# The prologue of a fused attention and MLP kernel: K and V from one combined weight, key norms from ScalarE, LayerNorm statistics and normalisations shared out anew over the engines

## The chip, the cores and the metric

The kernel runs on 1 core of one Trainium2 chip. The metric is the time of one execution in device microseconds (us), as the median of several executions. The profiler's own span of an execution is about 2 us shorter than the time measured for it, so spans are compared with spans and times with times.

Engine names: PE is TensorE (PEld its weight loads), ACT is ScalarE, DVE is VectorE, POOL is GpSimd, SP is SyncE.

## The reference

One LayerNorm feeds two branches, multi-query attention (32 query heads of width 16, one K and V head) and an MLP with GELU. Both are added to the input.

```python
S, D, H, Dh, F = 2048, 512, 32, 16, 1792           # bfloat16 inputs
def reference(A_x, A_wq, A_wk, A_wv, A_wo, B_x, B_w1, B_b1, B_w2, B_b2):
    def _A_ref(x, wq, wk, wv, wo):
        q = (x @ wq).reshape(B, S, H, Dh).transpose(0, 2, 1, 3)
        k = x @ wk
        v = x @ wv
        scores = einsum("bhqd,bkd->bhqk", q, k) * (Dh ** -0.5)
        p = softmax(scores, axis=-1)
        o = einsum("bhqk,bkd->bhqd", p, v)
        return o.transpose(0, 2, 1, 3).reshape(B, S, H * Dh) @ wo
    def _B_ref(x, w1, b1, w2, b2):
        return gelu(x @ w1 + b1) @ w2 + b2
    x = A_x
    xn = layernorm(x, eps=1e-5)                    # no scale, no shift
    return x + _A_ref(xn, ...) + _B_ref(xn, ...)
```

## The kernel before

The program is a list of operations with due dates. A scheduler, run when the kernel is built, fixes the order of the operations of each engine; semaphores come from the dependencies. So each engine has one fixed order. An operation that is ready still waits if the one ahead of it on its engine is not.

An eviction, below, is an operation that copies a result of TensorE from `pAll` (PSUM, the memory that its matmuls write to) to a tile such as `xnT` or `KT`. A filler is a matmul on zeros that only keeps TensorE busy. `bn_stats` are the statistics of a tile of rows, `ve_b` its variances (plus 1e-5), `rstd` their inverse square roots, `nmr` is -mean * rstd.

The work falls into a prologue and a stream. The prologue loads x, normalises it, transposes it into `xnT`, projects K and V for all 16 tiles of 128 rows and Q for the first group of heads. The stream then computes scores, exponentials and the products with V, block by block, with the other projections and the MLP in the gaps of TensorE. It starts with the first exponential (`exp`).

Softmax needs a number to subtract from the scores. The kernel uses a bound on |q|·|k|: the largest squared norm of a key (`R2`) times the squared norm of each query. The square root of the product is taken by halving the bits of the float, in the operation that writes `QT`. So no exp can start before all 16 tiles are normalised, transposed and projected to K.

The parts that the change touches (cuts marked):

```python
Q_DUE = 20.0
XN_ENG = "dddddddpdpdpdpdd"        # who normalises each tile: d VectorE, p GpSimd
LN_B = ((0,2),(2,3,1),(3,6),(6,7,1),(7,10),(10,11,1),(11,14),(14,16))  # ",1": statistics on ScalarE
# ... TR_B, K_B: batches of the transposes and of the K projections
dma("act", wk_s[:], ...); dma("act", wv_s[:], ...); dma("act", wq_s, ...)
# ...
def ln_batch(ts, on_act):
    # ... on_act: two passes of ScalarE over the tile (Identity and Square with accumulation)
    for ti in () if on_act else ts:
        dve(lambda e, ti=ti: e.bn_stats(stats[:, ti, :], x_sb[:, ti, :]), ...)
    for ti in () if on_act else ts:
        dve(lambda e, ti=ti: e.bn_aggr(mv[:, ti, :], stats[:, ti, :]), ...)
    if not on_act:
        dve(lambda e: e.tensor_scalar(ve_b[:, sl], mv[:, sl, 1], 1e-5, None, ALU.add), ...)
    act(lambda e: e.activation(std_b[:, sl], ve_b[:, sl], ACT.Sqrt), ...)
    dve(lambda e: e.reciprocal(rstd[:, sl], std_b[:, sl]), ...)
    for ti in ts:
        # VectorE if XN_ENG[ti] == "d", else GpSimd:
        # tensor_scalar(xn[:, ti % 8, :], x_sb[:, ti, :], mean, rstd, subtract, mult)

def x_T(ts, bk, eng):   # 4 transposes a tile on TensorE, then one copy of 128x1024 to xnT
    # ... ScalarE if eng == "a", else VectorE

def k_proj(ts, bk):     # wkp: wk, four times side by side
    for d in range(DT):
        mm(bank(bk)[:, 0:n], wkp[:, d, :, :].rearrange(...), xnT[:, d, c], d == 0, d == DT - 1, ...)
    act(lambda e: e.activation(KT[:, c], bank(bk)[:, 0:n], ACT.Identity, bias=krow[:, 0:1], scale=GAM), ...)

def k_max(ts, bk):      # squared key norms: square, matmul with ones, maximum
    dve(lambda e: e.tensor_tensor(sqk[:, i % 2, 0:n], KT[0:Dh, c], KT[0:Dh, c], ALU.mult), ...)
    mm(bank(bk)[:, 0:n], ones[0:Dh, :], sqk[:, i % 2, 0:n], True, True, ...)
    dve(lambda e: e.tensor_reduce(kmax[:, i:i + 1], bank(bk)[:, 0:n], AX.X, ALU.max), ...)

def wq_first():         # the weights of the first group of heads, an eighth of wq
    setup(lambda e: e.tensor_copy(wqp[:, :, 0:4, 0:Dh], wq_s[:, :, 0:64].rearrange(...)), due=9.0)  # GpSimd
# ... v_tiles: V of each tile from wv_s into pO (16 columns a tile)

# the tail: the bound, then the first QT
dve(lambda e: e.tensor_reduce(R2[:], kmax[:, 0:nkm[0]], AX.X, ALU.max), ...)
dve(lambda e: e.tensor_scalar(selrR[:], selr[:], R2[:, 0:1], 1.03, ALU.mult, ALU.mult), ...)
mm(bank(7), selrR[...], sqq[...], False, True, ...)                     # adds |q|^2 R2 to row 16
dve(lambda e: e.tensor_scalar(QT[:, hq, :].bitcast(i16), bank(7).bitcast(i32), isc[:, 0:1], ibi[:, 0:1],
                              ALU.mult, ALU.add), ...)                  # halves the bits: square root
# then V1, Vf (VectorE), the scaled copies of V and the rest of wqp (GpSimd), and the stream
```

Of the kernel before, what the change touches and what calls it, by code (L numbers as in the profile page):

```python
# [10 lines left out]
P = 128  # L11
# [31 lines left out]
LP = 154  # L43
# [7 lines left out]
KM_DUE = 5.0  # L51
Q_DUE = 20.0
XN_ENG = "dddddddpdpdpdpdd"
LN_B = ((0,2),(2,3,1),(3,6),(6,7,1),(7,10),(10,11,1),(11,14),(14,16))
TR_B = (((0,2),0,"a"),((2,4),1,"a"),((4,6),2,"a"),((6,8),3,"a"),((8,10),0,"a"),((10,12),1,"a"),((12,14),2,"a"),((14,16),3,"a"))
K_B = (((0, 4), 4, 5), ((4, 8), 4, 5), ((8, 12), 4, 5), ((12, 14), 4, 5), ((14, 16), 0, 1))
# [356 lines left out]
def bass_parallel_sum__grouped_kv_mqa__dense_activation_gelu__prompt_kernel(  # L413
# [34 lines left out]
    with ExitStack() as es:  # L448
# [8 lines left out]
        wk_s = sb([P, DT, Dh], bf, "wk_s")  # L457
        wv_s = sb([P, DT, Dh], bf, "wv_s")
# [23 lines left out]
        selrR = sb([P, 4, 32], bf, "selrR")  # L482
# [3 lines left out]
        nm = sb([P, NT], f32, "nm")  # L486
        scr = sb([P, D], bf, "scr")
# [4 lines left out]
        sqk = sb([Dh, 2, TBW], bf, "sqk")  # L492
        kmax = sb([P, 8], f32, "kmax")
# [63 lines left out]
        dma("act", wk_s[:], A_wk.rearrange("(k p) n -> p k n", p=P), "d_wk", w=["wk_s"], due=0.0)  # L557
        dma("act", wv_s[:], A_wv.rearrange("(k p) n -> p k n", p=P), "d_wv", w=["wv_s"], due=0.0)
# [6 lines left out]
        def setup(fn, r=(), w=(), occ=0.25, due=0.0, **kw):  # L565
# [17 lines left out]
        setup(lambda e: e.tensor_copy(wkp[:, :, :, 0:Dh], wk_s[:].unsqueeze(2).to_broadcast([P, DT, 4, Dh])),  # L583
              r=["wk_s", "wkp"], w=["wkp"], occ=0.45, due=2.0)

        sel_diag = bass.AP(sel8[:].tensor, sel8[:].offset, [list(sel8[:].ap[0]), [33, 8], [8, 4]])
# [4 lines left out]
        setup(lambda e: e.tensor_scalar(ibi[:], mrow[:], float(0x1fc00000) / 65536.0, None, ALU.mult),  # L591
              r=["mrow"], w=["ibi"], due=10.0)
# [6 lines left out]

        def land(ti):  # L600
            return 3.0 + 1.2 * (ti // 2) + 0.3 * (ti % 2)

        def ln_batch(ts, on_act):
            sl, b = slice(ts[0], ts[-1] + 1), ts[0]
            d = land(ts[-1])
            for ti in ts if on_act else ():
                act(lambda e, ti=ti: e.activation(scr[:], x_sb[:, ti, :], ACT.Identity, accum_out=sm[:, ti:ti + 1]),
                    r=[("x", ti)], w=["scr", ("sm", ti)], n=TBW + 200, due=land(ti))
            if on_act:
                setup(lambda e: e.tensor_scalar(mv[:, sl, 0], sm[:, sl], 1.0 / D, None, ALU.mult),  # L610
                      r=[("sm", ti) for ti in ts], w=[("mv", b, ti) for ti in ts])
                setup(lambda e: e.tensor_scalar(nm[:, sl], sm[:, sl], -1.0 / D, None, ALU.mult),
                      r=[("sm", ti) for ti in ts], w=[("nm", ti) for ti in ts])
            for ti in ts if on_act else ():
                act(lambda e, ti=ti: e.activation(scr[:], x_sb[:, ti, :], ACT.Square, bias=nm[:, ti:ti + 1],
                                                  accum_out=sm[:, ti:ti + 1]),
                    r=[("x", ti), ("nm", ti)], w=["scr", ("sm", ti)], n=TBW + 200, due=land(ti))
            if on_act:
                setup(lambda e: e.tensor_scalar(ve_b[:, sl], sm[:, sl], 1.0 / D, 1e-5, ALU.mult, ALU.add),
                      r=[("sm", ti) for ti in ts], w=[("ve", b)])  # L620
            for ti in () if on_act else ts:
                dve(lambda e, ti=ti: e.bn_stats(stats[:, ti, :], x_sb[:, ti, :]), r=[("x", ti)], w=[("st", ti)],  # L622
                    due=land(ti) + 1.0)
            for ti in () if on_act else ts:
                dve(lambda e, ti=ti: e.bn_aggr(mv[:, ti, :], stats[:, ti, :]), r=[("st", ti)], w=[("mv", b, ti)], n=130,
                    due=d + 1.0)
            if not on_act:
                dve(lambda e: e.tensor_scalar(ve_b[:, sl], mv[:, sl, 1], 1e-5, None, ALU.add),
                    r=[("mv", b, ti) for ti in ts], w=[("ve", b)], n=30, due=d + 1.1)
            act(lambda e: e.activation(std_b[:, sl], ve_b[:, sl], ACT.Sqrt), r=[("ve", b)], w=[("std", b)], n=70, due=0.0)  # L630
            dve(lambda e: e.reciprocal(rstd[:, sl], std_b[:, sl]), r=[("std", b)], w=[("rstd", b)], n=30, due=d + 1.2)
            for ti in ts:
                eng = XN_ENG[ti]
                if eng == "d":
                    dve(lambda e, ti=ti: e.tensor_scalar(xn[:, ti % 8, :], x_sb[:, ti, :], mv[:, ti, 0:1],
                                                         rstd[:, ti:ti + 1], ALU.subtract, ALU.mult),
                        r=[("x", ti), ("rstd", b), ("mv", b, ti)], w=[("u", ti % 8)], mode=4, due=land(ti) + 2.0)
                else:
                    add("pool", lambda e, ti=ti: e.tensor_scalar(xn[:, ti % 8, :], x_sb[:, ti, :], mv[:, ti, 0:1],  # L639
                                                                 rstd[:, ti:ti + 1], ALU.subtract, ALU.mult),  # L640
                        [("x", ti), ("rstd", b), ("mv", b, ti)], [("u", ti % 8)], occ=0.76, lat=0.15, due=land(ti) + 2.0)

        def x_T(ts, bk, eng):
            n = len(ts)
            pT = bank(bk)[:, 0:n * 256].bitcast(bf)
# [26 lines left out]
        nkm = [0]  # L672

        def k_max(ts, bk):
            c = slice(ts[0] * P, (ts[-1] + 1) * P)
            n = len(ts) * P
            u = land(ts[-1]) + KM_DUE
            i = nkm[0]
            nkm[0] += 1
            dve(lambda e: e.tensor_tensor(sqk[:, i % 2, 0:n], KT[0:Dh, c], KT[0:Dh, c], ALU.mult),  # L680
                r=[("KT", ti) for ti in ts], w=[("sqk", i % 2)], n=n, mode=2, due=u)
            mm(bank(bk)[:, 0:n], ones[0:Dh, :], sqk[:, i % 2, 0:n], True, True, r=["ones", ("sqk", i % 2)], w=[B(bk)],
               occ=0.216 * n / TBW, due=u)
            dve(lambda e: e.tensor_reduce(kmax[:, i:i + 1], bank(bk)[:, 0:n], AX.X, ALU.max), w=[B(bk), ("kmax", i)], n=n, due=u)
# [20 lines left out]
        def q_first_m(hq, bk):  # L705
            mm(bank(bk), selrR[:].rearrange("p a n -> p (a n)"), sqq[:, sq(hq), :], False, True,
               r=["selrR", ("h", sq(hq))], w=[B(bk)], skip=True, due=16.0)
            dve(lambda e: e.tensor_scalar(QT[:, hq, :].bitcast(i16), bank(bk).bitcast(i32), isc[:, 0:1], ibi[:, 0:1],
                                          ALU.mult, ALU.add),
                r=["isc", "ibi"], w=[B(bk), ("QT", hq)] + [("QTm", hq, j) for j in range(4)], due=16.0)  # L710

        def v_tiles(ts):
            for ti in ts:
                for d in range(DT):
                    mm(pO[:, ti * Dh:(ti + 1) * Dh], xnT[:, d, ti * P:(ti + 1) * P], wv_s[:, d, :], d == 0, d == DT - 1,
                       r=["wv_s", ("xnT", ti)], w=["O"], occ=0.06, due=land(ti) + 7.0, kind="v")
# [5 lines left out]
        steps = [(land(ts[1] - 1) + 2.0 * (ts[1] > 4), 0, "ln", ts) for ts in LN_B]  # L722
        steps += [(land(ts[1] - 1) + 4.0, 1, "tr", (ts, bk, eng)) for ts, bk, eng in TR_B]
        steps += [(land(ts[1] - 1) + 6.0, 2, "k", (ts, bk, bk2)) for ts, bk, bk2 in K_B]
        steps += [(land(4 * i + 3) + 6.5, 3, "v", i) for i in range(4)]
        steps.append((land(3) + 7.0, 4, "q", 0))
        for _, _, kind, a in sorted(steps, key=lambda s: s[:2]):
            if kind == "ln":
                ln_batch(list(range(*a[:2])), len(a) > 2)
            elif kind == "tr":  # L730
                x_T(list(range(*a[0])), a[1], a[2])
            elif kind == "k":
                k_proj(list(range(*a[0])), a[1])
                k_max(list(range(*a[0])), a[2])
            elif kind == "v":
                v_tiles(range(4 * a, 4 * a + 4))
# [5 lines left out]
        dve(lambda e: e.tensor_reduce(R2[:], kmax[:, 0:nkm[0]], AX.X, ALU.max), r=[("kmax", i) for i in range(nkm[0])],  # L742
            w=["R2"], n=30, due=16.0)
        dve(lambda e: e.tensor_scalar(selrR[:], selr[:], R2[:, 0:1], 1.03, ALU.mult, ALU.mult),
            r=["selr", "R2"], w=["selrR"], n=64, due=16.0)
        q_first_m(0, 7)
        dve(lambda e: e.tensor_copy(V1[:, 0, :, 0:Dh], pO[:, 0:NT * Dh].rearrange("p (t n) -> p t n", n=Dh)),
            r=["V1"], w=["O", ("V", 0)], n=256, due=22.0)
        dve(lambda e: e.tensor_copy(Vf[:], pO[:, 0:NT * Dh].rearrange("p (t n) -> p t n", n=Dh)), w=["O", "Vf"], n=256, due=22.1)
        for v, c in enumerate(SPL_C):  # L750
            setup(lambda e, v=v, c=c: e.tensor_scalar(V1[:, 1 + v, :, 0:Dh], Vf[:], c, None, ALU.mult),
                  r=["V1", "Vf"], w=[("V", 1 + v)], occ=0.45, due=20.0)

        setup(lambda e: e.tensor_copy(wqp[:, :, 4:H, 0:Dh], wq_s[:, :, 64:D].rearrange("p k (h n) -> p k h n", n=Dh)),
              r=[("u", i) for i in range(8, 12)] + ["wqp"], w=["wqp"], occ=2.7, due=19.0, after=[pr.writer["R2"]])
        setup(lambda e: e.tensor_scalar(sel8R[:], sel8[:], R2[:, 0:1], 1.03, ALU.mult, ALU.mult),
# [374 lines left out]
```

## Time and profile before

| | before |
|---|---|
| time, median of the first 3 executions (lowest to highest; a fourth is added below) | 830.98 us (830.92 to 833.13) |
| span of the profiled execution | 830.4 us |
| first exp starts at | 34.25 us |
| from there to the end | 796.15 us |

The page of the profile shows what the stream is bound by. In its first part a line gives busy time, share of the span and number of instructions of each engine. In its groups the columns are line, engine, operation, output from input, shapes and count, then the busy time and the mean ns of one, then the engine's idle time ahead of them and what ended it.

```profile
PE 797.3 (96%) x9287; PEld 251.5 (30%) x9287; DVE 748.6 (90%) x1443; ACT 787.6 (95%) x741; POOL 26.2 (3%) x52
...
L813 ACT ACTIVATE E<-pAll 128x1024 bf16<-128x1024 f32 (+1 forms) x683 | 747.3, 1340 | 18.9 <-PE pAll L794 16.1
```

ScalarE spends 747 of its 788 busy us in exp, and over the whole span it is idle for only 18.9 us ahead of them, 16.1 us of that waiting for scores. From the first exp on ScalarE has little idle time to win, and the change touches nothing there. What can be won is an earlier first exp.

The chain of waits of the kernel before, cut to the first 36 us, shows what the prologue waits for. Each line is a start, a duration and the work that the next line was released by (or followed on the same engine).

```profile
1.81 5.37 DMA x_sb<-in_A_x_dram
...
15.36 2.24 POOL ub L639
...
19.89 4.28 POOL ub L639 x2
...
29.38 0.48 ACT KT L669
...
31.59 0.44 DVE selrR L744
...
32.73 0.82 DVE QT L708
...
33.60 0.63 PE pAll L794 x3
```

Three normalisations by GpSimd (`ub L639`) lie on the chain for 6.5 us. The end is a sequence of single steps on alternating engines, from the eviction of the last keys at 29.38 to the scores at 33.60. The groups by shape of the same 36 us give the cost of one normalisation on each engine:

```profile
L622 DVE BATCH_NORM_STATS2 stats<-x_sb 128x6 f32<-128x512 bf16 x13 | 8.6, 678 | 2.4 <-DMA x_sb<-in_A_x_dram 2.4
L639 POOL TENSOR_SCALAR ub<-x_sb,mv,rstd 128x512 bf16<-128x512 bf16 x4 | 8.6, 2147 | 0.8 <-DVE mv L625 0.8
...
L635 DVE TENSOR_SCALAR ub<-x_sb,mv,rstd 128x512 bf16<-128x512 bf16 x12 | 4.7, 418 | 0.0
```

The same operation takes 2147 ns on GpSimd and 418 ns on VectorE.

### The profile page before, as it was taken

What the parts mean: (1) busy time and instruction counts of PE and PEld (TensorE: products, weight loads), DVE (VectorE), ACT (ScalarE), POOL (GpSimd) and SP (SyncE); (2) the same over time, 40 slices, a digit from 0 to 9 for tenths busy, and PEclk for the clock granted to TensorE, in tenths of its full rate; (3) what the DMA queues carried; (4) which work ended last, traced back from release to release, by engine and by line L of the source; (5) the groups of instructions that cost most, each with busy time, mean ns of one, the idle gap of its engine ahead of it and who ended that gap; (6) DMA issues with size and microseconds to landing.
All of it is one profiled execution on the core that took longest, in us unless ns stands there. A gap on an engine that the chain in (4) does not pass through costs nothing.

```text
span 830.4 us, 21532 instructions
## 1 busy us (share of the span) xinstructions
PE 797.3 (96%) x9287; PEld 251.5 (30%) x9287; DVE 748.6 (90%) x1443; ACT 787.6 (95%) x741; POOL 26.2 (3%) x52
## 2 busy tenths in 40 slices
PE   6799999999999999999999999999999999999998
PEld 4322222232233233332222233223332322223233
DVE  7499999988999779999999859999999868999995
ACT  6699999999999999999999998999999899999993
POOL 6600000000000000000000000000000000000000
PEclk9599999999999999999999999999999999999999
DMA  9000000000000000000000000000000000000000
GB/s 305 1 28 15 16 15 15 12 6 14 15 15 28 22 9 16 15 15 15 9 9 21 22 21 22 16 2 15 15 15 15 28 21 22 2 15 15 15 15 27
DMA packets 23975, 19.08 MB, mean 23 GB/s; under 512 B 12369, under 2 KB 19402, under 8 KB 23882
## 3 DMA queue, kind: packets, MB, share of 16 engines
q1 hardware_dynamic: 22298, 17.17, 6.8%
q8 instruction: 73, 1.20, 0.6%
q10 hardware_dynamic: 1584, 0.56, 0.3%
q14 instruction: 20, 0.16, 0.1%
HBM read 14.98 MB, written 2.35 MB: 21 GB/s over the span
## 4 chain that ended last, share of the span: by engine, by line
ACT 44%; PE 42%; DVE 11%; POOL 1%; issue 1%; DMA 1%; SPq 0%; DVEq 0%
ACT E L813 43%; PE pAll L834 16%; PE pAll L794 12%; PE pAll L544 11%; DVE Dt L845 3%; DVE Dt L830 3%; ACT ub L936 2%; PE pAll L1092 1%; PE pAll L538 1%; DVE hb L922 1%; POOL ub L639 1%; DMA x_sb<-in_A_x_dram 1%; DVE stats L622 1%; DVE ub L938 0%; DVE ub L935 0%
## 5 line engine op out<-in xcount | busy, mean ns | idle before, releaser
L813 ACT ACTIVATE E<-pAll 128x1024 bf16<-128x1024 f32 (+1 forms) x683 | 747.3, 1340 | 18.9 <-PE pAll L794 16.1
L834 PE MATMUL pAll<-Dt,V 128*32 128x512 bf16 x2090 | 349.2, 383 | 0.5
L830 DVE TENSOR_SCALAR Dt<-pAll 128x512 int16<-128x512 f32 x418 | 282.5, 686 | 47.8 <-PE pAll L794 46.1
L834 PE MATMUL pAll<-E,V 128*32 128x512 bf16 x1630 | 295.1, 386 | 0.4
L845 DVE TENSOR_SCALAR Dt<-Dt 128x1536 int16<-128x1536 int16 (+2 forms) x600 | 286.1, 525 | 2.8 <-PE pAll L544 1.7
L794 PE MATMUL pAll<-QT,KT 32*128 32x512 bf16 x2048 | 268.0, 386 | 17.1 <-ACT E L813 9.8
L794 PEld LDWEIGHTS pAll<-QT,KT 32*128 32x128 bf16 x2048 | 67.6, 91 | 296.3 <-ACT E L813 257.1
L834 PEld LDWEIGHTS pAll<-Dt,V 128*32 128x32 bf16 x2090 | 97.7, 95 | 92.5 <-issue 41.7
L544 PE MATMUL pAll<-w_sb,ub 128*32 128x512 bf16 x896 | 99.7, 383 | 0.0
L834 PEld LDWEIGHTS pAll<-E,V 128*32 128x32 bf16 x1630 | 73.6, 94 | 69.1 <-issue 48.0
L544 PE MATMUL pAll<-wop,oT 128*32 128x512 bf16 x512 | 81.4, 382 | 0.0
L544 PE MATMUL pAll<-xnT,w_sb 128*32 128x512 bf16 x896 | 72.4, 383 | 0.8 <-DVE hb L922 0.4
L1092 PE MATMUL pAll<-xnT,zeros 128*32 128x512 bf16 x492 | 52.3, 383 | 0.0
L922 DVE TENSOR_SCALAR hb<-pAll,b1T 128x512 bf16<-128x512 f32 x56 | 41.7, 744 | 4.7 <-PE pAll L834 3.4
L544 PE MATMUL pAll<-xnT,wqp 128*32 128x512 bf16 x496 | 41.4, 391 | 0.4 <-DVE hb L922 0.3
L544 PEld LDWEIGHTS pAll<-w_sb,ub 128*32 128x32 bf16 x896 | 26.3, 95 | 24.3 <-issue 14.7
L936 ACT ACTIVATE ub<-ub 128x1536 bf16<-128x1536 bf16 (+1 forms) x20 | 31.3, 1566 | 0.0
L544 PEld LDWEIGHTS pAll<-xnT,w_sb 128*32 128x32 bf16 x896 | 19.5, 95 | 29.0 <-issue 13.8
L544 PEld LDWEIGHTS pAll<-wop,oT 128*32 128x32 bf16 x512 | 22.7, 95 | 11.9 <-issue 5.6
L696 DVE CAST QT<-pAll 128x512 bf16<-128x512 f32 x32 | 21.8, 683 | 2.7 <-PE pAll L544 2.7
L858 DVE COPY Of<-pAll 128x512 f32<-128x512 f32 x31 | 21.2, 682 | 1.2 <-PE pAll L834 1.2
L869 DVE TENSOR_TENSOR oT<-Of,rbc 128x512 bf16<-128x512 f32 x31 | 21.3, 686 | 0.0
(100 smaller groups left out, 283.4 us busy)
## 6 DMA issues: line engine op xcount, KB each, us to landing
rbc<-rden_rows SPq DMA_DIRECT2D x124, 64.0 KB, 2.0
w_sb<-in_B_w_dram SPq DMA_DIRECT2D x2, 1792.0 KB, 12.7
x_sb<-in_A_x_dram SPq DMA_DIRECT2D x8, 256.0 KB, 6.5
out_dram<-x_sb SPq DMA_DIRECT2D x16, 128.0 KB, 1.7
QT<-mT SPq DMA_DIRECT2D x60, 2.0 KB
ub<-in_A_wq_dram ACTq DMA_DIRECT2D x1, 512.0 KB, 7.3
wop<-in_A_wo_dram SPq DMA_DIRECT2D x4, 128.0 KB, 2.8
den<-Of SPq DMA_DIRECT2D x31, 8.0 KB
```

Of the source, the lines that this page charges most:

```text
L544: add("pe", lambda e, c=c, j=j: e.matmul(o[c, :], l[:, c], rh, start=start, stop=stop, tile_position=(0, 32 * j)), r, [(k, j) for k in w] ...
L696: dve(lambda e: e.tensor_copy(QT[:, hq, :], bank(bk)), w=[B(bk)] + [(B(bk), j) for j in range(4)] + [("QT", hq)] + [("QTm", hq, j) for j i ...
L794: ins = e.matmul(o, l, rh, start=True, stop=True, tile_position=(q0, 0))
L813: exps.append(act(lambda e: e.activation(E[:, s0:s0 + na, :], bank(b0, na).rearrange("p (a n) -> p a n", a=na), ACT.Exp, scale=LN2 / 128.0 ...
L830: dve(lambda e: e.tensor_scalar(Dt[:, KZ, s, :], bank(bk), float(127 * 128) + SPL_D, SPL_MIN, ALU.add, ALU.max), w=[B(bk), ("D", s, KZ)], ...
L834: add("pe", lambda e, a, b: e.matmul(pO[32 * j:32 * j + 32, :], V1[:, v, kt, :], rhs, start=a, stop=b, tile_position=(0, 32 * j)), r=r + [ ...
L845: dve(lambda e, k=k: e.tensor_scalar(Dt[:, k, s0:s0 + n, :], Dt[:, KZ, s0:s0 + n, :], float(SPL_K[k]), None, ALU.add), r=[("D", s0 + i, KZ ...
L858: dve(lambda e: e.tensor_copy(Of[:, i, :], pO), w=["O", ("Of", i)], allow=0.0)
L869: onorm[gg] = dve(lambda e: e.tensor_tensor(oT[:, gg % NOT, :], Of[:, i, :], rbc[:, i, :], ALU.mult), r=[("Of", i)] + [("rbc", i, j) for j ...
L922: dve(lambda e: e.tensor_scalar(hb[:, ft % 6, :], pM, b1T[:, ft:ft + 1], None, ALU.add), r=["b1T"], w=M4 + [("h", ft % 6)], allow=ev)
L936: act(lambda e: e.activation(uu, uu, ACT.Tanh, scale=GELU_K), r=uk, w=uk, n=c, allow=al - 0.5, kind="tanh")
L1092: pr.filler = lambda e, j, o: e.matmul((pO if o else pM)[32 * j:32 * j + 32, :], zeros[:, 0:32], xnT[:, 0, 0:TBW], start=not o, stop=not o ...
```

## The change

The intent is an earlier first exp, by five means: no normalisation on GpSimd (six go to ScalarE, ten to VectorE); all statistics by VectorE's `bn_stats`, in four of the five batches aggregated by eight small GpSimd operations a batch (tiles 1 to 3 still by VectorE's `bn_aggr`); K and V of a tile from one weight `wvk` of 32 columns, so that the key norms can be had from these columns by a ScalarE Square and a short reduction; a bound that enters the first `QT` only through its bias `ibi`, so that the matmul with `selr` need not wait for it; and the table of Sqrt loaded ahead of the data. The core of the diff (cuts marked):

```diff
-XN_ENG = "dddddddpdpdpdpdd"
-LN_B = ((0,2),(2,3,1),(3,6),(6,7,1),(7,10),(10,11,1),(11,14),(14,16))
+XN_ENG = "adaaddddaddddaad"
+LN_B = ((0, 1, 'p'), (1, 4, 'd'), (4, 7, 'p'), (7, 10, 'p'), (10, 16, 'p'))
 # ... Q_DUE 20 -> 16; two evictions of TR_B from 'a' to 'd'; K_B in smaller batches
-dma("act", wk_s[:], ...)
-dma("act", wv_s[:], ...)
+dma("act", wvk[:, :, Dh:2 * Dh], A_wk...)
+dma("act", wvk[:, :, 0:Dh], A_wv...)
 # ...
+act(lambda e: e.activation(dum[:], krow[:], ACT.Sqrt, scale=-1.0), ..., due=-1.0)   # loads the table
 # ... in ln_batch, for how == "p", after bn_stats on VectorE:
+setup(lambda e: e.tensor_tensor(sm[:, sl], st[:, :, 1], st[:, :, 4], ALU.subtract), ...)   # GpSimd
+setup(lambda e: e.tensor_tensor(nm[:, sl], st[:, :, 2], st[:, :, 5], ALU.add), ...)
+ # ... four more up to ve_b, two for the mean
 act(lambda e: e.activation(std_b[:, sl], ve_b[:, sl], ACT.Sqrt), ...)
 dve(lambda e: e.reciprocal(rstd[:, sl], std_b[:, sl]), ...)
+# ... nmr = -mean * rstd, two GpSimd operations, where a tile of the batch is normalised by ScalarE
-add("pool", lambda e, ti=ti: e.tensor_scalar(xn[:, ti % 8, :], x_sb[:, ti, :], mv[:, ti, 0:1], ...))
+act(lambda e: e.activation(xn[:, ti % 8, :], x_sb[:, ti, :], ACT.Identity, bias=nmr[:, ti:ti + 1],
+                           scale=rstd[:, ti:ti + 1]), ...)
 # ... k_max:
-dve(... tensor_tensor(sqk, KT, KT, mult)); mm(ones, sqk); dve(... tensor_reduce(kmax, 128x512, max))
+act(lambda e: e.activation(ksq[:, a:b, :], kk, ACT.Square), ...)          # kk: the K columns of 14 or 2 tiles
+dve(lambda e: e.tensor_reduce(kmax[:, a:b], ksq[:, a:b, :], AX.X, ALU.add), ...)
 # ... v_tiles: rhs wv_s -> wvk, 32 columns a tile
 # ... the tail:
-dve(... tensor_reduce(R2, kmax, max)); dve(... selrR = selr * R2 * 1.03)
+dve(... tensor_reduce(kmx, kmax, max)); add("pe", ... transpose(bank(3)[0:1, 0:P], kmx, ident_f))
+dve(... tensor_reduce(kmr, bank(3)[0:1, 0:P], max)); mm(bank(3)[:, 256:257], crow[0:1, :], kmr[0:1, :], ...)
+dve(lambda e: e.tensor_scalar(ibi[:], bank(3)[:, 256:257].bitcast(i32), 0.5 / 65536.0, mrow[:, 0:1], ...))
```

## The prediction

> **What bounds the kernel now.** The page: ScalarE busy 95%, TensorE 96%, VectorE 90%, and the chain that ended last is 43% exp (L813). From the first exp on, the kernel is a steady stream: the windows view has ScalarE busy 98 to 99% from 40 us to 800 us. Its first exp starts at 34.25 us of 830.4 (timeline), so 796 us lie behind it. The change touches only what lies before (LP has no effect while FIN_F is 0; the choice of VectorE tiles is computed from costs that stay). The whole gain can only be an earlier first exp.
>
> **What bounds the prologue.** x has landed by about 12 us (issues from 0.8 to 5.2 us, 3.0 to 7.1 us to landing; DMA 0.13 busy after 20 us). The chain of waits then runs over VectorE statistics to two GpSimd normalisations, 15.4-17.6 and 19.9-24.2 us: 2147 ns each (groups by form), four of them, where VectorE takes 411 ns for one tile. TensorE transposes and evictions wait for them (6.9 us in the waits view). The tail from the last xnT eviction (28.67) to the first exp takes 5.6 us: K, KT eviction, square, ones matmul, reduce, R2, selrR (0.43), matmul (0.61, clock 0.50), QT (0.81), scores (0.65).
>
> **What the change does, costed.**
> 1. GpSimd normalisations go (4 x 2.15, about 6.5 us of them on the chain); ScalarE gets six of about 0.63 us (the 128x512 Identity took 0.625), VectorE ten at 0.36-0.41.
> 2. All 16 bn_stats go to VectorE (0.60-0.65 each back to back), against 13; ScalarE loses three two-pass statistics (about 1.7 us each); 13 of 16 bn_aggr (0.15-0.18) become small GpSimd ops, 8 a batch at about 0.17-0.2, six of them (1.2 us) before the Sqrt.
> 3. KT squares and maximum reductions on VectorE (about 1.9 + 2.9 us) go; a ScalarE Square and a short reduce remain.
> 4. Two xnT evictions move to VectorE, about 1.2 us each (estimate from the 128x512 PSUM cast, 0.66). The Skill's "VectorE: DVE Perf Modes" (Mode 2x_2P) says PSUM has one read port, so no two-port speed-up.
> 5. One Sqrt table load (1.28 us) moves before the data.
>
> VectorE is then the limit: 10 stats + 4 norms + 2.4 evictions + 2.6 small work and QT = about 19 us from 3.8 us, with about 1 us waiting for x. I estimate the last bn_stats at 18 to 19 us, the last rstd at 20-20.8, norms and two xnT evictions behind it on ScalarE, the last xnT at 24-24.8. The new tail: K and V matmuls 1.1, Square 0.3, two reduces 0.4, transpose 0.3, reduce 0.2, matmul 0.2, ibi 0.15, QT 0.85, scores 0.65: 4.2 to 4.5, little shorter than 5.6, as it has more hops. First exp at 28.2 to 29.3: 5 to 6 us earlier. All of this is on the critical path, nothing of it behind the first exp. V copies now follow QT, so V variants come perhaps 1 us later relative to the first exp; the first PV has slack. The stream's order changes with the new start times: worth +-1.5 us either way.
>
> **Predicted: 825.8 us, 8 in 10 within 822.5 to 829.3.** Faster by over 2%: 0.01; within 2%: 0.98; slower by over 2%: 0.01.
>
> **What would show it.** First exp at about 28.8 us in the timeline; no 2 us GpSimd gaps before transposes; VectorE nearly full from 7 to 18 us; R2 chain of about 2 us; stream from the first exp to the end again 796 us.
>
> **What would make it wrong.** The Exp table load (1.28 us) placed ahead of the last Square; GpSimd's small ops queued behind its 1.38 us memset; static order stalling VectorE on ScalarE; a slower V variant or wqp stalling the first tiles; a stream that reorders for the worse and gives the gain back.

## The result, and the profile after

| | before | after |
|---|---|---|
| time, median of 4 executions (lowest to highest) | 831.54 us (830.92 to 833.13) | 828.33 us (827.99 to 829.22) |
| ratio, with its 95% interval | | 0.996 (0.9943 to 0.9978) |
| span of the profiled execution | 830.4 us | 826.4 us |
| first exp starts at | 34.25 us | 30.40 us |
| from there to the end | 796.15 us | 796.0 us |

A ratio is the mean time of one kernel's fast runs over that of the other's of the same rounds, so it is not quite the ratio of the medians. It says 0.4% faster, and by the rule of 2% the two kernels are the same.

In the two profiled executions nearly the whole gain (3.85 of 4.0 us of span) is an earlier first exp, with a stream as long as it was. The prediction had named this mechanism but forecast 5 to 6 us. The next table takes the prologue apart; its times are read from the timeline of each profile.

| us | before | after | forecast |
|---|---|---|---|
| last `bn_stats` ends | 19.71 | 17.40 | 18 to 19 |
| last `rstd` starts | 24.42 | 21.15 | 20 to 20.8 |
| last `xnT` eviction ends | 28.67 | 25.51 | 24 to 24.8 |
| first exp starts | 34.25 | 30.40 | 28.2 to 29.3 |
| last statistics to last `rstd` | 4.71 | 3.75 | 1.8 to 2.0 |
| last `rstd` to last `xnT` | 4.25 | 4.36 | about 4.0 |
| last `xnT` to first exp | 5.58 | 4.89 | 4.2 to 4.5 |

The statistics were earlier than forecast. The time was lost after them, most of it between the last statistics and the last `rstd`. The forecast column of the lower three rows is worked out from the upper ones and from the sum of the tail in the prediction.

The page of the kernel after, its busy line and its exp:

```profile
PE 794.9 (96%) x9292; PEld 250.4 (30%) x9294; DVE 746.1 (90%) x1425; ACT 784.7 (95%) x733; POOL 23.7 (3%) x79
...
L854 ACT ACTIVATE E<-pAll 128x1024 bf16<-128x1024 f32 (+1 forms) x683 | 747.0, 1333 | 16.8 <-PE pAll L835 14.2
```

The stream is unchanged: 683 exps, 747 us. The chain of waits of the kernel after, cut to the first 36 us, answers to the one of before:

```profile
1.88 7.30 DMA ub<-in_A_wq_dram
...
9.23 0.40 POOL wqp L752
9.63 0.26 POOL nmr L663
...
9.91 2.22 ACT ub L674 x3
...
20.34 0.69 ACT KT L706
21.02 0.10 ACT std_b L657
21.13 0.02 issue
21.15 0.20 DVE rstd L658
...
22.18 1.50 ACT ub L674 x2
23.68 1.83 ACT xnT L692 x2
...
31.19 1.63 POOL wqp L796
```

The GpSimd normalisations are gone from it. Its end no longer runs through the bound and the first `QT` but through GpSimd's copies of V and of wq, to which e7 below comes back. (This is the chain of what ended last; the first exp, at 30.40, still waits for the bound and the first `QT`.) Two more things are new. First, the chain starts at the load of wq instead of x. GpSimd copies the first slice of wq (`wqp L752`) as soon as it has landed, but in GpSimd's fixed order this copy stands ahead of the small operation `nmr L663` that the first ScalarE normalisation needs. So the first normalisation by ScalarE waits until 9.91 for a weight that it does not use, and TensorE waits 4.8 us for its first transpose (the waits view has it as the longest wait of TensorE in the prologue). Second, the last Sqrt (`std_b L657`) stands on ScalarE directly behind an eviction of keys (`KT L706`). Its own input had been ready for long. GpSimd's timeline has the operation that made it (start, duration, engine, line, operation; in brackets, where there is one, the idle time ahead and what ended it):

```profile
18.75 0.20 POOL L653 TENSOR_TENSOR ve_b<-sm,nm 128x6 bf16<-128x6 f32 x1
```

ScalarE's timeline has the Sqrt itself, `std_b`, and what stands ahead of it:

```profile
20.34 0.69 ACT L706 ACTIVATE KT<-pAll,krow 128x512 bf16<-128x512 f32 x1 [1.26 <-PE pAll L544]
20.92 0.20 ACT L657 ACTIVATE std_b<-ve_b 128x6 bf16<-128x6 bf16 x1
```

The variances were there at 18.95 us. ScalarE was free from 19.07 on, but sat idle for 1.26 us waiting for the K matmuls of tiles 4 to 7, evicted them, and took the Sqrt at 20.92: 2.0 us late. These matmuls could start only at 19.28: ScalarE evicted the transposes of tiles 6 and 7 from 18.05 to 19.07, and those transposes stood on TensorE behind slow matmuls. TensorE's timeline in the same stretch:

```profile
15.09 1.49 PE L544 MATMUL pAll<-xnT,wkp 128*128 128x512 bf16 x3 [0.22 <-issue]
...
16.58 1.01 PE L544 MATMUL pAll<-xnT,wqp 128*128 128x512 bf16 x2
...
19.28 1.02 PE L544 MATMUL pAll<-xnT,wkp 128*128 128x512 bf16 x4
```

Two matmuls of 512 columns take 1.01 us at 16.58 and four take 1.02 us at 19.28. TensorE was at half speed for the first part of its work (the expectations call this cold). The Trainium skill, "TensorE: Matmul & The Clock Gate" (What's actually happening), says that TensorE drops to half its clock after an idle window of about 3.4 us and needs a busy one to come back. This trace agrees: 4.8 us of idle time lie just before, and the durations are halved later.

Of the groups of the first 36 us, these three answer to those of before:

```profile
L692 ACT ACTIVATE xnT<-pAll 128x1024 bf16<-128x1024 bf16 x6 | 5.9, 1014 | 0.4 <-PE pAll L687 0.3
...
L674 ACT ACTIVATE ub<-x_sb,nmr,rstd 128x512 bf16<-128x512 bf16 x6 | 4.5, 803 | 1.8 <-POOL nmr L663 1.8
...
L694 DVE COPY xnT<-pAll 128x1024 bf16<-128x1024 bf16 x2 | 1.4, 683 | 0.0
```

A ScalarE normalisation took 803 ns (0.75 back to back), where I had taken 0.63; an `xnT` eviction on VectorE took 683 ns, where I had taken 1.2 us. Both come back below.

### The profile page after: what moved, and what is told of

Read it like the earlier page. It is cut to its first block, busy times and chain, and to the rows that moved or that the text cites. A ratio compares the mean times of both kernels' runs of the same rounds, so it can differ in the third digit from the quotient of the medians.

```text
span 826.4 us, 21561 instructions
## 1 busy us (share of the span) xinstructions
PE 794.9 (96%) x9292; PEld 250.4 (30%) x9294; DVE 746.1 (90%) x1425; ACT 784.7 (95%) x733; POOL 23.7 (3%) x79
## 4 chain that ended last, share of the span: by engine, by line
ACT 51%; PE 39%; DVE 7%; DMA 1%; issue 1%; POOL 1%; ACTq 0%; POOLq 0%; DVEq 0%
ACT E L854 48%; PE pAll L875 15%; PE pAll L835 12%; PE pAll L550 10%; DVE Dt L886 2%; ACT ub L977 2%; DVE Dt L871 2%; PE pAll L1133 1%; DMA ub<-in_A_wq_dram 1%; PE pAll L544 1%; DVE hb L963 1%; ACT ub L674 0%; ACT xnT L692 0%; DVE ub L976 0%; POOL V L793 0%
## 5 line engine op out<-in xcount | busy, mean ns | idle before, releaser
L550 PE MATMUL pAll<-xnT,w_sb 128*32 128x512 bf16 x896 | 70.5, 383 | 0.6 <-DVE hb L963 0.5
L550 PEld LDWEIGHTS pAll<-xnT,w_sb 128*32 128x32 bf16 x896 | 19.1, 95 | 29.3 <-issue 13.8
```

The costliest lines, as they stand in the source:

```text
L550: add("pe", lambda e, c=c, j=j: e.matmul(o[c, :], l[:, c], rh, start=start, stop=stop, tile_position=(0, 32 * j)), r, [(k, j) for k in w] ...
```

## The experiments

The theory after reading the profile (A): the missing gain lies in the order of GpSimd and ScalarE and in the slow TensorE. That is, wq's copy delays the first normalisations, the Sqrt stands behind a late eviction, and both meet a TensorE at half speed. The expectations use letters of their own: "Theory A" and "Theory B" of e2 and e3 are the two halves of (A) here, wq's copy with the slow TensorE and the place of the Sqrt, and "Theory C" of e10 is about transfers. Two rivals: (B) the gain does not come from the redistribution as a whole but from taking the normalisations off GpSimd alone; (C) the first exp is not what sets the time, and the stream gives back what the prologue wins.

The experiments use a helper that moves one operation in the finished order of its engine, and a loop that adds zero matmuls, so that nothing else of the order changes (e1 and e6 change a constant instead, and the scheduler orders the whole program anew):

```python
def put_after(pr, op, target):      # the order only; dependencies and semaphores follow from it
    pr.ops.remove(op); pr.ops.insert(pr.ops.index(target) + 1, op)
```

All times are set against executions of the kernel before on the same chip. All twelve runs gave correct results. The last two columns come from one profile each.

| experiment | median us (n) | before, median us | ratio (95%) | first exp | first exp to end |
|---|---|---|---|---|---|
| the change (first runs) | 828.33 (4) | 831.54 | 0.996 (0.9943 to 0.9978) | 30.40 | 796.0 |
| e1 no GpSimd normalisations | 832.78 (6) | 832.43 | 1.0 (0.9981 to 1.002) | 31.16 | 798.74 |
| e2 wq copy later | 828.03 (6) | 832.43 | 0.995 (0.9929 to 0.9971) | 29.38 | 796.12 |
| e3 last Sqrt first | 828.7 (6) | 832.43 | 0.9954 (0.9933 to 0.9974) | 28.90 | 797.4 |
| e4 TensorE kept warm | 827.08 (6) | 832.43 | 0.9933 (0.9911 to 0.9954) | 28.66 | 797.44 |
| e5 these three together | 827.89 (5) | 831.86 | 0.9948 (0.9933 to 0.9964) | 30.50 | 796.0 |
| e6 e1 with earlier filler | 830.98 (6) | 831.86 | 0.9983 (0.9966 to 1.0001) | 30.37 | 795.53 |
| e7 rest of wq copied early | 829.43 (6) | 831.86 | 0.9968 (0.9952 to 0.9984) | 31.38 | 795.52 |
| e8 all four, and a warm tail | 828.54 (5) | 831.86 | 0.9957 (0.9941 to 0.9974) | 29.13 | 796.67 |
| e9 the change again | 828.36 (5) | 832.56 | 0.996 (0.9944 to 0.9976) | 30.15 | 795.95 |
| e10 wq loaded after x | 826.95 (5) | 832.56 | 0.9939 (0.9926 to 0.9953) | 29.70 | 797.1 |
| e11 e10 with warm TensorE | 826.65 (5) | 832.56 | 0.9936 (0.9923 to 0.9949) | 28.83 | 796.07 |
| e12 the best of all | 826.99 (6) | 832.94 | 0.9923 (0.9904 to 0.9942) | 27.61 | 797.39 |

The rows e1 to e4, e5 to e8 and e9 to e11 each shared a chip. A caution for the whole table: most of the ratios differ by less than their intervals are wide. Where one kernel is set against another below, the argument rests on stretches in the profiles, and each of those is one execution.

### e1: the kernel before, with the GpSimd normalisations alone undone

```diff
-XN_ENG = "dddddddpdpdpdpdd"
+XN_ENG = "dddddddddddddddd"
```

> The kernel before with one part of the change alone: the four GpSimd normalisations (2147 ns each) go to VectorE (411 ns each). If they were the bound of the prologue, the first exp comes at 29 to 31 us instead of 34.25 and the total falls by 3 to 5 us, so that this alone is worth as much as the whole change. If VectorE was as much a bound as GpSimd, the first exp comes only 1 to 2 us earlier and the total falls by 1 to 2 us.

Measured: 832.78 us, ratio 1.0, so no gain at all. Yet the first exp came at 31.16 us, 3.1 us earlier than before, and only 0.76 us later than with the whole change. The stream took 2.6 us longer. The windows view of this run shows where (start:end and length, then busy time and count of PE, PEld, DVE, ACT and POOL, then the granted clock of TensorE, the share of the DMA and its GB/s):

```profile
56.00:60.00 4.00, 2.78 (x24) 0.78 (x22) 4.00 (x10) 4.00 (x6) 0.00 (x0) 1.00 0.01 2
60.00:64.00 4.00, 2.98 (x17) 0.56 (x14) 4.00 (x10) 4.00 (x5) 0.00 (x0) 0.60 0.00 1
64.00:68.00 4.00, 4.00 (x43) 1.43 (x43) 3.11 (x6) 2.18 (x2) 0.00 (x0) 0.54 0.04 6
```

ScalarE's timeline has the two gaps:

```profile
66.55 1.45 ACT L813 ACTIVATE E<-pAll 128x1536 bf16<-128x1536 f32 x1 [1.82 <-PE pAll L834]
68.79 3.71 ACT L813 ACTIVATE E<-pAll 128x1536 bf16<-128x1536 f32 x3 [0.79 <-PE pAll L794]
```

TensorE was busy for only 2.8 to 3.0 us of each 4 us from 56 to 64 us, its clock was then 0.54 to 0.60, it fell behind, and ScalarE lost 1.82 and 0.79 us waiting for it. So rival B holds for the prologue: the normalisations alone give four fifths of the earlier first exp (3.1 of 3.85 us). For the total it does not hold, as the ratio is 1.0. And rival C has something in it: an earlier start can be given back in the stream, in this execution by a stretch of half clock.

### e6: e1, with filler matmuls allowed 20 us earlier

The kernel fills gaps of TensorE in the stream with zero matmuls, in the schedule's reckoning from 60 us on. This run lets them begin at 40 us.

```diff
-FILL_FROM = 60.0
+FILL_FROM = 40.0
```

> The kernel before with all normalisations on VectorE, as in the first experiment (first exp 3.1 us earlier, total the same, because the clock fell to 0.50 between 61 and 67 us and exp stood idle 2.6 us), and the existing TensorE filler allowed from model time 40 us instead of 60. If the half clock near 60 us took the gain, it is gone from the trace and the total is 2 to 3 us below before. If the gain was lost for another reason (the order of the stream), the total stays within 1 us of before although the clock is full.

Measured: the profiled execution took 828.01 us, first exp at 30.37, a stream of 795.53, no stretch of half clock at 60 us, and ScalarE idle for 0.16 us between 60 and 80 us where e1 had 2.61. But the other five executions took 830.81 to 831.89 us, and the ratio is 0.9983. So the profile shows what the earlier first exp was worth in one execution without the dip. The others have no profile, and what they lost is not known. As a remedy it is inconclusive.

### e2: wq's copy moved behind the small operations of tiles 1 to 3

```diff
+    put_after(pr, wq_copy, nmr[1])          # GpSimd's order only
```

> The changed kernel; on GpSimd alone the copy of wq's first columns is issued after the two small ops that the first ScalarE normalisations wait for, instead of ahead of them; every other engine keeps its order. Theory A (the copy waits for wq's transfer until 9.2 us and holds up the queue behind it; TensorE idles 4.8 us and goes cold): the first normalisation starts at about 8.2 instead of 9.9 us, the clock in 12 to 20 us rises, the first exp comes 1.2 to 1.8 us earlier than 30.40, total about 1.5 us less. Theory B (the last Sqrt stands behind a KT eviction on ScalarE, and that sets the end): first exp moves by less than 0.4 us.

Measured: the operation `nmr` no longer waits for the weight, and the first normalisation starts at 8.33 instead of 9.91. In GpSimd's timeline the copy is now the only one to wait for it:

```profile
9.22 0.48 POOL L766 COPY wqp<-ub 128x256 bf16<-128x256 bf16 x1 [0.27 <-DMA ub<-in_A_wq_dram]
```

The first exp came 1.0 us earlier, at 29.38, between the two ranges that were expected. Of the 0.87 us by which the last statistics were earlier, 0.37 us is a tile of x that VectorE could start on at 8.43 instead of 8.80, which this edit does not explain. The stretch from the last statistics to the last `rstd` stayed at 3.83 us. The queueing is shown, then, but it is worth less than 1 us, and it is not the missing term.

### e3: the last Sqrt put ahead of the key eviction

```diff
+    put_after(pr, KT_eviction[4], sqrt[10])     # ScalarE's order only
```

> The changed kernel; on ScalarE alone the last batch's Sqrt is issued ahead of the eviction of KT for tiles 4 to 7, behind which it waited 2.0 us (18.94 to 20.92). Theory B: rstd comes at about 19.4 instead of 21.15, the first exp 1 to 1.8 us earlier. Theory A: TensorE is cold and its queue reaches the last transposes only at 21.8 whatever ScalarE does, so the first exp moves by at most 0.5 us.

Measured: from the last statistics to the last `rstd` it is 1.91 us instead of 3.75, about the 1.8 to 2.0 us that the prediction had counted. In the timeline below the Sqrt starts 0.03 us after its variances (18.34 us), and the key eviction comes 0.68 us after the Sqrt: the wait that made up the term is gone. How long it would have been in this execution is another matter, since TensorE was less slow here (the first Q matmuls took 0.59 us, not 1.01). The first exp came at 28.90, 1.5 us earlier, but 0.61 us of that is an earlier end of the statistics, which the edit does not explain. And 1.15 us came back in the next stretch, from `rstd` to the last `xnT` (5.51 instead of 4.36). ScalarE's timeline of this run shows the next one in the queue:

```profile
18.37 0.21 ACT L671 ACTIVATE std_b<-ve_b 128x6 bf16<-128x6 bf16 x1 [0.46 <-POOL ve_b L667]
19.05 0.69 ACT L720 ACTIVATE KT<-pAll,krow 128x512 bf16<-128x512 f32 x1 [0.46 <-PE pAll L557]
20.51 0.47 ACT L720 ACTIVATE KT<-pAll,krow 128x256 bf16<-128x256 f32 x1 [0.78 <-PE pAll L557]
20.88 1.51 ACT L688 ACTIVATE ub<-x_sb,nmr,rstd 128x512 bf16<-128x512 bf16 x2
```

The last two ScalarE normalisations stand behind the eviction of tiles 8 and 9, and this one waits for TensorE too. The Sqrt went free only to meet the next late matmul. The time of the kernel (0.9954) is not told apart from that of the change.

### e4: 40 zero matmuls before the first transpose

```diff
+    insert 40 zero matmuls on TensorE behind the last filler of the prologue
```

> The changed kernel; 40 more zero matmuls of 256 columns on TensorE between the last filler (6.0 us) and the first transpose (10.8 us), nothing else moved. If the cold clock (0.50 to 0.66 between 8 and 20 us) is what makes the KT eviction and so the last Sqrt late, the clock there becomes 1.0 and the first exp comes 0.8 to 1.5 us earlier; if the late normalisations set the pace and TensorE only waits for them, less than 0.3 us. It may also go cold again by itself before 16 us, as transposes and waits do not fill it: then the clock column shows it.

Measured: TensorE is busy up to the first transpose (10.80 us), and the first K and Q matmuls have full speed, as in this line of its timeline:

```profile
15.29 0.59 PE L566 MATMUL pAll<-xnT,wqp 128*128 128x512 bf16 x2
```

The same two took 1.01 us in the profile of the change. The keys are evicted at 18.81, the Sqrt starts at 19.40 instead of 20.92, and the stretch to the last `rstd` is 2.46 us, with nothing else in the order changed. First exp at 28.66, 1.74 us earlier. The Sqrt now starts 0.50 us after its variances instead of 1.97 us. So the slow clock is the larger part of the reason why the eviction ahead of the Sqrt was late. The ratio, 0.9933, is among the lowest.

### e5: e2, e3 and e4 together

```diff
+    put_after(pr, wq_copy, nmr[1])
+    put_after(pr, KT_eviction[4], sqrt[10])
+    insert 24 zero matmuls on TensorE behind the last filler of the prologue
```

> The changed kernel with the three single moves together (wq copy later on GpSimd, last Sqrt first on ScalarE, TensorE kept warm with 24 zero matmuls ahead of the first transpose). Alone they brought the first exp from 30.40 to 29.38, 28.90 and 28.66. If each removes a different wait, the first exp comes at about 27.2 to 27.8; if they are three handles on one wait (cold TensorE behind late normalisations), at about 28.4 to 28.7. The total follows only as far as the stream behind it stays at 796: it was 797.4 in two of the three, with the clock at half for 3 us near 60 us in one of them.

Measured: first exp at 30.50 us, far from the expected one. In this profile one tile of x arrived late: VectorE began it at 9.49 us after 1.04 us of waiting (8.80 with the change). From 12 to 16 us TensorE was at half clock again. The Sqrt was free, but `rstd` then stood on VectorE behind the evictions of Q and `xnT`, the first of which had waited 1.10 us for the slow matmuls, so that the stretch to the last `rstd` is 2.64 us; and from there to the last `xnT` it is 5.38 us, much as in e3. So the slow TensorE is met again on another engine. In this profile the three remedies did not add up; whether they would with x in time, this run can't say (e12, which has moves of these three kinds and more, comes to 27.61). The miss also brought up something that neither theory had: the arrival of x, which e10 tests.

### e7: the rest of wq copied before the copies of V

In the chain of the kernel after, one more piece lies behind the tail: four scaled copies of V (GpSimd, 0.86 us each) and behind them the copy of the rest of wq (1.63 us, done at 32.83), which the next Q projections wait for. This run moves that copy ahead.

```diff
+    put_after(pr, rest_of_wq_copy, nmr[10])     # GpSimd's order only
```

> The changed kernel; the GpSimd copy of wq's remaining columns (1.68 us) is issued right after the last nmr op, at about 22 us, where GpSimd idles 5.6 us, instead of behind four V copies at 31.1. If the first q projection's wait for it (0.86 us on TensorE, then 0.5 us of idle exp near 35.5) costs time, the stream from first exp to end shortens by 0.3 to 0.8 us and the first exp stays at 30.4. If the stream absorbs it, or GpSimd's port use slows VectorE's normalisations at 21.4 to 22.8 us, no gain, and the last xnT comes later.

Measured: the stream was 0.5 us shorter (795.52), its first 48 exps without a gap. But the first exp came 0.98 us later, at 31.38, and 0.94 us of that lie between the last `rstd` and the last `xnT`. The chain of waits of this run has three normalisations on it:

```profile
21.64 2.43 DVE ub L685 x3
```

GpSimd's timeline has the copy beside them:

```profile
22.15 1.76 POOL L810 COPY wqp<-ub 128x1792 bf16<-128x1792 bf16 x1
```

Three VectorE normalisations took 2.43 us beside GpSimd's copy (four take 1.38 us in the profile of the change). The Trainium skill, "SBUF — State Buffer" (SBUF: two separate sides), says that VectorE, in the modes that use two ports, and GpSimd share a pair of ports to this memory, taken for a whole instruction, and that the other engine waits meanwhile. This run agrees: one of the four normalisations took 1766 ns where their median is 412 ns, beside a copy of 1.76 us, and the four together took 1.36 us more (2.74 against 1.38).

### e8: all four moves, and zero matmuls in the tail

```diff
+    the edits of e5 and e7
+    3 zero matmuls behind the transpose of kmx, 9 behind the matmul with kmr
```

> All four moves, and 12 zero matmuls on TensorE between the last ops of the chain to the score bound, so that the stream starts at full clock (it is at 0.50 from about 30 to 41 us in every kernel so far). First exp at 27.2 to 28.5 as in the run of three, the clock in 28 to 40 us above 0.9 if the fillers suffice, stream 795.5 to 796.5 if no half-clock stretch comes near 57 to 62 us; total 824 to 825.5, the best so far. If the cold start costs nothing, as exp has no idle in most of it, the total is that of the run of three.

Measured: first exp at 29.13 us, later than expected, and TensorE at full clock from 28 to 40 us, where every other profile has 0.50 to 0.58 from 32 to 36 us. The first 12 exps have no gap. But two gaps, of 1.09 and 0.27 us, came at 43 to 46 us instead, with a clock of 0.60 in the windows view:

```profile
40.00:44.00 4.00, 3.48 (x32) 0.99 (x29) 0.35 (x2) 3.22 (x3) 0.00 (x0) 0.60 0.12 34
```

The time is 828.54 us, no better than that of the change and outside the expected range. In this profile, then, the slow stretch came after the warm start instead of before it; one profile cannot say that the one caused the other. (The expectation's "in every kernel so far" is not exact: in e3 the clock was 1.00 from 36 us on.)

### e9: the change again

No edit, on the chip of e10 and e11.

> The changed kernel itself again, beside the same runs of before as the next two, to see how far one execution's profile carries. Total 3 to 4.5 us below before. First exp between 29.5 and 31.5 us; where it differs from 30.40, the arrival of x (tile 6 was waited for until 8.80) and of wq (9.18) should differ by as much, and the stretch from the last bn_stats to the last rstd should again be 3 to 4 us with the clock at half between 8 and 19 us.

Measured: 828.36 us, 0.996, first exp 30.15, stretches of 3.63, 4.36 and 4.89 us. A second profile of the change thus agrees with the first. One line is worth a look. In this profile the windows view gives a clock of 1.00 from 8 to 24 us, but TensorE's timeline has the slow durations:

```profile
16.46 1.01 PE L544 MATMUL pAll<-xnT,wqp 128*128 128x512 bf16 x2
```

The column can miss a slow stretch; the durations of known matmuls do not.

### e10: wq loaded behind x on the same queue

The eight loads of x (256 KB each) and the load of wq (512 KB) ran side by side. Here wq is issued on SyncE's queue after the last x; its copy on GpSimd moves back accordingly.

```diff
-dma("act", wq_s, ...)
+dma("sp", wq_s, ...)                        # behind the eight loads of x
+    put_after(pr, wq_copy, mean[7])
```

> The changed kernel; wq's transfer (512 KB) is issued after the eight of x instead of alongside them, and its first GpSimd copy stands behind the small ops of tiles 7 to 9. Theory C (transfers compete: x arrives late because wq shares the queue's bandwidth): VectorE's wait for tile 6 ends before 8.4 us, the last bn_stats ends at 16.0 to 16.5 instead of 17.40, first exp 28.6 to 29.4. Rival: VectorE's own work sets the last bn_stats, and the gain is only that of the wq copy standing out of the way (first exp 29.4, as measured for that alone). If wq now lands later than 14 us, the first q projection waits and takes it back.

Measured: x lands in 4.6 us (median from issue to landing) instead of 6.6, VectorE waits for one x tile only, and the last statistics end at 16.26 us, 1.1 us earlier than with the change. From there the old troubles remain: TensorE is slow, and the stretch to the last `rstd` is 4.20 us. The first exp comes at 29.70 us. The kernel takes 826.95 us, against 828.36 us for the change on the same chip; the intervals of the two ratios overlap. The expectation's rival is not ruled out: in e10 the copy of wq stands out of the way as in e2, and e2 alone had its last statistics at 16.53 and its first exp at 29.38.

### e11: e10 with 24 zero matmuls

```diff
+    the edits of e10
+    insert 24 zero matmuls on TensorE behind the last filler of the prologue
```

> The same with 24 zero matmuls ahead of the first transpose. If the clock at half is the second cause, the stretch from the last bn_stats to the last rstd falls from 3.75 to about 2.5 us as in the run with TensorE kept warm, first exp 27.5 to 28.3 and a total of 823.5 to 825.5; if the clock falls anyway between 12 and 16 us, as it did with 24 zero matmuls in the run of three, the stretch stays above 3 us.

Measured: first exp at 28.83 us, span 824.9, time 826.65 us, all short of the hoped-for branch of the expectation. The stretch to the last `rstd` is 3.56 us, as the other branch had it: the Sqrt still started about 1.8 us after its variances, behind the key eviction, and TensorE's clock was 0.61 from 12 to 16 us.

### e12: what was learned, in one kernel

```diff
+    the edits of e11, and 6 more zero matmuls behind the sixth V matmul
+    put_after(pr, KT_eviction[4], sqrt[10])
+    put_after(pr, KT_eviction[8], normalisation[14])
+    rest_of_wq_copy: behind VectorE's last xnT eviction (a dependency added)
```

> The version that the runs point to: wq's transfer after x's, 24 + 6 zero matmuls on TensorE ahead of the first and third groups of transposes, the last Sqrt ahead of the KT eviction of tiles 4 to 7 and the last two ScalarE normalisations ahead of the KT eviction of tiles 8 and 9 (in the run with the Sqrt alone the last xnT came 1.15 us later after rstd, because they stood behind it), and the rest of wq's copy on GpSimd behind VectorE's last xnT copy, where VectorE is idle, so that it doesn't slow the normalisations as it did in the run where it stood beside them (+0.94 us). Last rstd 18.0 to 18.6 us, last xnT 22.8 to 23.6, first exp 27.4 to 28.3, stream 795.4 to 797.4, total 6 to 8 us below before, about 1 us below the run of wq after x kept warm. If the transposes on TensorE's queue (K of tiles 8 and 9 ahead of them) set the end, the last xnT stays near 24.

Measured: first exp at 27.61 us, as early as expected, 6.6 us earlier than before. The stretch from the last statistics to the last `rstd` is 2.01 us. In ScalarE's timeline the Sqrt starts as soon as the variances are there, and the eviction of keys comes after it:

```profile
17.91 0.21 ACT L697 ACTIVATE std_b<-ve_b 128x6 bf16<-128x6 bf16 x1 [1.26 <-POOL ve_b L693]
18.02 0.67 ACT L746 ACTIVATE KT<-pAll,krow 128x512 bf16<-128x512 f32 x1
19.04 1.52 ACT L714 ACTIVATE ub<-x_sb,nmr,rstd 128x512 bf16<-128x512 bf16 x2 [0.35 <-POOL nmr L703]
```

The ratio is 0.9923, the lowest: about 6.4 us off the mean of the kernel before, nearly twice the gain of the change. It beats both kernels, though not by 2%. Its interval does not meet that of the change (0.9904 to 0.9942 against 0.9944 to 0.9976, on different chips), but it does meet those of e2 to e5, e8, e10 and e11. Of the 6.6 us at the first exp, the profiled execution kept 5.4 (830.4 to 825.0), since its stream took 797.39 us, with a slow stretch here too, in the windows view:

```profile
56.00:60.00 4.00, 2.91 (x25) 0.76 (x28) 3.35 (x7) 3.73 (x5) 0.00 (x0) 0.72 0.03 6
```

### The slow stretches of the stream, over all runs

From 80 us on, ScalarE's gaps have the same sizes in the profiles that I compared, to within 0.02 us, some shifted by one slice, up to about 780 us (before, after, e1, e6, e12; for example 3.01 us between 640 and 660 us in each). The differences arise between the first exp and 80 us. There, some profiles show TensorE at a lower clock for some us and others do not. Over the 113 executions (13 sets of runs of the change and the experiments, four of the kernel before), taken as deviations from the mean of each group, the span falls by 0.29 us for each 0.001 of mean granted clock (correlation -0.72). The section of the Trainium skill's page on TensorE that was cited above says that the window in which TensorE's activity is counted runs freely and that the slow part varies from run to run. That fits the scatter of 1 to 5 us within one kernel. The correlation alone does not say which is cause and which is effect. In the profiles of e1, e3, e8, e10 and e12 the gaps of ScalarE come within or just after the slow stretch. No run took the clock away with all else the same, so this is the likely reading and not a proof.

## Why the prediction was right, and where it was wrong

**Right: the total and its mechanism.** 825.8 us was forecast with 822.5 to 829.3; 828.33 was measured, and the chance of 0.98 was on "within 2%". The gain is an earlier first exp: 796 us from there to the end was forecast, 796.0 measured. That the total fell into its range is in part luck. The range of 6.8 us was wide beside the forecast gain of 5.2 us (830.98 to 825.8; measured 3.3 by the ratio), and two errors partly cancelled: the last statistics came 0.6 to 1.6 us earlier than forecast, the way from there to the last `rstd` took 1.75 to 1.95 us longer.

**Wrong in size: "I estimate the last bn_stats at 18 to 19 us, the last rstd at 20-20.8".** This is the term of the sum that failed. The distance, 1.8 to 2.0 us in the prediction, measured 3.75 us. The prediction summed the costs of operations (six small GpSimd operations, 1.2 us, and a Sqrt). The GpSimd operations did take 1.5 us from 17.48 to 18.95. What it left out was the place of the Sqrt in ScalarE's order: behind an eviction of keys that waited for matmuls at half speed. e3 takes the Sqrt out of that place, and the term is 1.91 us. e4 leaves it there and makes the matmuls fast, and the term is 2.46 us. e12 does both, among other things, and has 2.01 us. e2, which removes the other wait that the profile showed (GpSimd behind wq's load), leaves the term as it was, at 3.83 us. So do the other runs that keep the Sqrt's place and in which TensorE was slow: 3.63 (e7), 4.20 (e10) and 3.56 us (e11). In e5 and e8, with the Sqrt free and TensorE slow, it is 2.64 and 2.56 us, since `rstd` then stands in a queue on VectorE. The prediction's list of dangers had this one in general words ("static order stalling VectorE on ScalarE"), but gave it no size.

**Wrong in size: the tail, 4.2 to 4.5 us.** It measured 4.89. I had listed the steps of the bound. The chain has two evictions of keys on ScalarE (0.37 and 0.47 us) and VectorE's copies of V between these steps, again because of a fixed order.

**Wrong in size: ScalarE's normalisation, 0.63 us.** It took 0.80 (0.75 back to back). I had read 0.625 us from an Identity without operands from memory. The Trainium skill, "ScalarE: Activation LUTs" (What ACT_TABLE_LOAD costs), gives 186 ns plus 0.833 ns an element, and about 93 ns for each operand that is read from memory (bias and scale here). With two of them and 512 elements that is an estimate of 799 ns. The trace has 803.

**Wrong in size, in favour: `xnT` on VectorE, 1.2 us.** It took 0.683 us. I had leaned on the statement that PSUM gives no two-port mode. The page that I cited, "VectorE: DVE Perf Modes" (Why PSUM operands drop a tier), says what is left: 16-bit data can still go two at a time through one port. The trace agrees, with 683 ns for 1024 bf16 elements and 682 ns for 512 f32 elements (`Of` in the profile of before). It did not bring the first exp forward by itself: the two evictions start at 19.49 and 22.67 us, behind the last `bn_stats`. The forecast had summed them, 2.4 us, into VectorE's work as a whole; that this is why it had the last statistics too late is likely, but not tested.

**On the attribution.** The prediction spread the gain over five parts of the change. e1 shows that taking the normalisations off GpSimd (there all to VectorE) gives 3.1 of the 3.85 us at the first exp, and e6 with the same string and earlier fillers reached 30.37 us. The other parts together gave 0.76 us in the profiles. That is no proof that they are idle, as they change the order of everything.

**What stays open.** Why e1 and e6 have so much less in the median than the change has, at nearly the same first exp. The mean clock does not explain it: averaged over the executions it is 0.985 in e1 and 0.989 in e6, against 0.987 and 0.989 in the two sets of the change, while e6's spans are on average 1.5 to 1.9 us longer. The profiled execution of e6 was its fastest by far, so its page does not show what the others met. Whether the half clock at the very start of the stream costs anything: e8 removed it and the gaps came later. And how often each kernel's prologue runs at half clock, as there is one profile of each (two of the change).

## What to carry to other kernels

In a program with a fixed order on each engine, sum the waits and not the operations: for each step on the chain, look up what stands directly ahead of it on its engine and what that one is waiting for. A small operation of the critical path (a Sqrt of 0.2 us, an `nmr` of 0.3 us) behind an eviction or a copy that waits for a matmul or a load costs as much as that wait. Before rewriting a prologue in five ways, measure the single line that removes its slowest operation, and look at the stream after it, because a few microseconds won at the start can be lost there: e1 won 3.1 us at its first exp and gained nothing in time.

## What the Trainium skill lacked or had wrong

- "GPSIMD Engine Reference" (Elementwise — side-by-side cycle accounting) has a factor of 1.96 between GpSimd and VectorE, for an fp32 `tensor_tensor`. It has no measured time for a bf16 `tensor_scalar` from one input; its section Engine selection only says that one-input operations run roughly at line rate, which does not fit. Here the normalisation of 128x512 took 2147 ns on GpSimd and 418 ns on VectorE, a factor of 5.1.
- "ScalarE: Activation LUTs" (What ACT_TABLE_LOAD costs) puts a switch of tables at 2.66 us, 1283 ns of it the load and the rest a drain. The load took 1.28 us here, but the drain does not show: in the profile after, the operation before the last load ends at 28.22 us, the load runs from 28.24 to 29.52, and the next operation starts at 29.54.
- "TensorE: Matmul & The Clock Gate" (Seeing it yourself) warns that clock events are unreliable and advises a check against a sum of throttled time, which does not say where in a trace TensorE was slow. In e9 the clock column read 1.00 while two matmuls of 512 columns took 1.01 us instead of 0.59. Comparing the durations of equal matmuls shows it in the timeline.
